# First half of batch 0's k loaded as float32 on another queue and cast by its permutes; permutes of batch 1 ordered later

**Chip, cores, metric.** One core of a Trainium2 chip. Times are device microseconds (us) of one execution.

## The reference

```python
kv  = k^T @ v                          # per batch and head: 8 batches, 8 heads, 576 rows, 64 columns
out = q @ kv                           # per batch and head
x   = out / sqrt(mean(out**2, -1) + 1e-6) * g_norm      # laid out as [8, 576, 512]
xn  = (x - mu) / sqrt(var + 1e-6) * g_ln                    # over the 512 columns
y   = x + relu(xn @ w_ch1) @ w_ch2                          # 512 -> 2048 -> 512
```

(Shortened to formulas. All inputs and the output are float32; the kernel multiplies in bfloat16.)

## The kernel before

It is written as a list of steps. Each has an engine, an estimated duration, a key and dependencies; a small scheduler in Python simulates the engines and fixes the order in which each engine's instructions are issued. So an edit of a duration or a `lag` changes the order of instructions, not their waits. The parts that matter (cuts marked):

```python
PARTS = ((0, 4), (4, 8))           # halves of the 8 heads
SPLIT_STORE = (23, 25)
...
def ready(s): ...                  # d.done + (s.lag if d is a DMA): when the plan thinks s may run
...
# SyncE queue: two small rows of scales first
row = [add("SP", 0.4, 1.4, -99, [], lambda x=x, f=f: nc.sync.dma_start(scales[:, f], ...)) ...]
# PE spreads them over 128 partitions: the two "scale matmuls"
def spread(f): nc.tensor.matmul(ps, lhsT=ones, rhs=scales[:, f], ...)
...
# GpSimd (POOL) queue: loads that cast float32 to bfloat16, one behind the other
pool_load(("k", 0, 0), load_kv(kb, k, 0, 0, 4), rate6)        # k, heads 0 to 3
pool_load(("v", 0, 0), load_kv(vb, v, 0, 0, 4), rate6)        # v, heads 0 to 3
pool_load(("k", 0, 4), load_kv(kb, k, 0, 4, 8), rate6)
pool_load(("q", 0, 0, 0), load_slot(qp[0], q, 0, 0, 0, 4), rate1)
pool_load(("v", 0, 4), ...); pool_load(("v", 0, 6), ...)      # v, the last four heads
...
pool_load(("q", 0, 1), ...); load_w(0, 1)                     # first weight of w_ch1
pool_load(("q", 0, 2), ...); load_w(1, 1)                     # q slot 2, second weight
...
# permutes: [row, head, t, d] -> [row, t, head, d], bf16 to bf16
for i, (h0, h1) in enumerate(PARTS):
    k0p.append(add("DVE", ..., load["k", 0, h0], lambda ...: k_permute(nc.vector, 0, h0, h1)))
...
# PE fills its waiting time ahead of the first feed-forward matmul with dummy matmuls (idle_ps)
```

The order on PE is: dummy matmuls, scale matmuls, the kv groups of batch 0 (three, as v arrives), q transposes, out, transposes of x, then the feed-forward matmuls.

## Time and profile before

| kernel before | value |
|---|---|
| time, median of 3 | 293.01 us (292.86 to 293.27) |
| span of the profile | 291.03 us |
| first kv group starts | 7.57 us |
| first feed-forward matmul starts | 17.24 us |
| last matmul ends | 287.57 us |

The text below shows the lines that carry this. Two lines that it does not show turn out to matter. They are from the timeline of PE in the kernel before (start, duration, engine, line, operation, count), just behind the first feed-forward group:

```profile
18.30 0.68 PE L579 MATMUL xT_ps<-identity,xc 128*128 128x128 bf16 x4
18.82 3.74 PE L629 MATMUL mm_ps<-xT,w 128*128 128x128 bf16 x64
```

and from the view of one tile, the second weight (the one `w` load issued in that stretch; the last line is issue to landing):

```profile
L354 POOL DMA_DIRECT2D w<-in_moe_w_ch_dram x1: 782/782/782, 9.6 to 9.6; - x1
...
DMA to landing us min/median/max: 9.1/9.1/9.1
```

The weight was issued at 9.63 and landed at 18.73; the second feed-forward group starts at 18.82. No wait is listed there, and yet that group could start at most 0.09 us earlier.

### The profile page before, as it was taken

The page shows a single profiled execution, that of the slowest core. Times are in us where ns is not written, and L with a number is a line of the kernel's source. Part 1 is how long each engine was busy: PE and PEld are TensorE (multiplying, and loading weights), DVE is VectorE, ACT ScalarE, POOL GpSimd, SP SyncE. Part 2 cuts the span into 40 slices and gives each one's busy share as a digit, 9 for nine tenths or more (in the row PEclk, how much of TensorE's full clock was granted, in tenths as well). Part 3 has the DMA queues.
Part 4 walks back from the last instruction along what each step waited for, and adds up shares of the span by engine and source line. Part 5 has one row for each costly group of instructions (what it writes and reads, how often), then busy time and mean ns, then how long its engine had stood idle before and what let it go on. Part 6 is the DMA issues. An engine that isn't in the chain of part 4 may idle for free.

```text
span 291.0 us, 5193 instructions
## 1 busy us (share of the span) xinstructions
PE 283.3 (97%) x2046; PEld 162.0 (56%) x2074; DVE 165.0 (57%) x362; ACT 142.5 (49%) x288; POOL 66.3 (23%) x93
## 2 busy tenths in 40 slices
PE   8899999999999999999999999999999999999995
PEld 6779845977645445444544445444544444444444
DVE  2596139487973997556755775477557755320022
ACT  2379954788756512761276126612761177016400
POOL 8974221008209005404060405000000000000000
PEclk9999999999999999999999999999999999999999
DMA  6999999959999989996999299912101310120012
GB/s 95 186 199 205 204 199 181 240 94 96 183 220 92 171 117 186 142 190 127 169 93 199 62 202 108 182 55 93 54 18 56 90 54 18 58 91 15 2 72 73
DMA packets 108716, 35.60 MB, mean 122 GB/s; under 512 B 87187, under 2 KB 104467, under 8 KB 108692
## 3 DMA queue, kind: packets, MB, share of 16 engines
q0 software_dynamic: 72624, 18.35, 65.9%
q1 hardware_dynamic: 35828, 16.79, 25.7%
q8 instruction: 16, 0.26, 0.4%
q10 hardware_dynamic: 240, 0.13, 0.2%
q14 instruction: 8, 0.07, 0.1%
HBM read 36.70 MB, written 9.44 MB: 159 GB/s over the span
## 4 chain that ended last, share of the span: by engine, by line
PE 85%; DMA 7%; POOL 6%; issue 1%; ACT 0%; DVE 0%; POOLq 0%
PE mm_ps L663 41%; PE mm_ps L644 33%; DMA qb<-in_q_dram 7%; PE mm_ps L629 5%; PE out_ps L484 3%; PE kv_ps L461 2%; POOL qp L270 1%; POOL w L354 1%; POOL vb L249 1%; POOL kb L249 1%; PE xT_ps L579 1%; POOL w L356 1%; PE qT_ps L420 0%; ACT qp L400 0%; POOL identity masks.py:197 0%
## 5 line engine op out<-in xcount | busy, mean ns | idle before, releaser
L663 PE MATMUL mm_ps<-w,m 128*128 128x512 bf16 (+2 forms) x592 | 128.1, 367 | 0.7
L644 PE MATMUL mm_ps<-xT,w 128*128 128x512 bf16 x436 | 100.0, 379 | 0.6
L651 ACT ACTIVATE m<-mm_ps 128x512 bf16<-128x512 f32 x112 | 66.8, 598 | 50.7 <-PE mm_ps L644 48.4
L663 PEld LDWEIGHTS <-m 128*128 128x128 bf16 x608 | 57.2, 98 | 60.6
L644 PEld LDWEIGHTS <-w 128*128 128x128 bf16 x448 | 43.1, 98 | 48.8
L519 DVE TENSOR_REDUCE ss<-sq 128x8 f32<-128x512 f32 (+1 forms) x37 | 24.8, 669 | 48.1 <-ACT sq L510 48.0
L670 DVE SCALAR_TENSOR_TENSOR x<-mm_ps,rstd,x 128x512 f32<-128x512 f32 (+2 forms) x38 | 27.3, 720 | 40.5 <-PE mm_ps L663 40.5
L510 ACT ACTIVATE sq<-out_ps 128x512 f32<-128x512 f32 (+1 forms) x37 | 21.6, 585 | 45.5 <-PE out_ps L484 45.5
L629 PE MATMUL mm_ps<-xT,w 128*128 128x128 bf16 x512 | 30.5, 219 | 0.0
L629 PEld LDWEIGHTS <-w 128*128 128x128 bf16 x512 | 29.2, 98 | 0.7
L572 DVE SCALAR_TENSOR_TENSOR xc<-x,mv,gl 128x512 bf16<-128x512 f32 (+1 forms) x38 | 27.3, 723 | 1.2
L514 DVE TENSOR_TENSOR xg<-out_ps,gn 128x512 f32<-128x512 f32 x34 | 23.2, 683 | 0.2
L636 ACT ACTIVATE m<-mm_ps 128x512 bf16<-128x512 f32 x32 | 18.5, 600 | 3.1 <-PE mm_ps L629 2.9
L751 POOL COPY mark<-xT 128x1 bf16<-128x1 bf16 x15 | 6.4, 425 | 56.8 <-DMA xT<-xc 51.2
L523 ACT ACTIVATE rms<-ss,eps_attn 128x8 f32<-128x8 f32 (+1 forms) x37 | 11.1, 301 | 14.5 <-DVE ss L519 14.4
L550 DVE TENSOR_TENSOR x<-xg,inv 128x512 f32<-128x512 f32 x24 | 16.6, 692 | 0.8
L566 DVE BATCH_NORM_STATS2 stats<-x 128x6 f32<-128x512 f32 x24 | 16.6, 690 | 0.5
L484 PEld LDWEIGHTS <-qT 128*128 128x128 bf16 x160 | 11.4, 98 | 6.5 <-ACT qT L400 0.2
L484 PE MATMUL out_ps<-kv_pack,qT 128*128 128x128 bf16 x160 | 14.5, 219 | 0.3
L472 DVE CAST kv_pack<-kv_ps 64x256 bf16<-64x256 f32 x14 | 5.9, 422 | 11.9 <-PE kv_ps L461 11.8
L461 PEld LDWEIGHTS <-kp 128*128 128x128 bf16 (+1 forms) x168 | 10.4, 100 | 2.4 <-DMA vb<-in_v_dram 0.4
L277 POOL DMA_DIRECT2D qp<-in_q_dram x5 | 11.2, 2235 | 0.8 <-issue 0.8
(69 smaller groups left out, 182.9 us busy)
## 6 DMA issues: line engine op xcount, KB each, us to landing
out_dram<-x SPq DMA_DIRECT2D x30, 256.0 KB, 2.9
w<-in_moe_w_ch_dram POOLq DMA_DIRECT2D x8, 512.0 KB, 12.0
vb<-in_v_dram POOLq DMA_DIRECT2D x6, 512.0 KB, 10.9
kp<-in_k_dram POOLq DMA_DIRECT2D x5, 512.0 KB, 8.5
qp<-in_q_dram POOLq DMA_DIRECT2D x5, 512.0 KB, 10.1
out_dram<-x SPq DMA_DIRECT2D x10, 128.0 KB, 2.3
qb<-in_q_dram POOLq DMA_DIRECT2D x2, 512.0 KB, 18.4
qp<-in_q_dram POOLq DMA_DIRECT2D x10, 64.0 KB, 9.1
```

The lines of the kernel that those rows point to most:

```text
L484: nc.tensor.matmul(o3[:, hp, :], lhsT=att[b]["qT"][:, 4 * t + hp, :], rhs=kv_pack[b % 3][:, hp, :], start=(i == 0), stop=(i == len(bs) - 1))
L510: nc.scalar.activation(sq[:, h0:h1, :], st[n]["ps", h0][:, h0:h1, :], func=AF.Square)
L514: nc.vector.tensor_mul(xg[:, h0:h1, :], st[n]["ps", h0][:, h0:h1, :], gn.to_broadcast([128, h1 - h0, D]))
L519: nc.vector.tensor_reduce(ss[:, h0:h1, :], st[n]["sq"][:, h0:h1, :], axis=AX.X, op=ALU.add)
L550: nc.vector.tensor_mul(x, xg, inv)
L572: nc.vector.scalar_tensor_tensor(xc[:, f0:f1], in0=st[n]["x"][:, f0:f1], scalar=blk[m]["mv"][:, i, 0:1], in1=gl[:, f0:f1], op0=ALU.subtrac ...
L629: nc.tensor.matmul(ps[:, d, :], lhsT=w1[c][:, kk, d * 128:(d + 1) * 128], rhs=blk[m]["xT"][:, kk, i * 128:(i + 1) * 128], start=(kk == 0), ...
L636: nc.scalar.activation(st[n]["m1"][:, c, :, :], st[n]["m1ps", c], func=AF.Relu)
L644: nc.tensor.matmul(ps, lhsT=w1[c][:, kk, d * 128:(d + 1) * 128], rhs=blk[m]["xT"][:, kk, :], start=(kk == 0), stop=(kk == nKm - 1))
L651: nc.scalar.activation(blk[m]["m1", c][:, d, :], blk[m]["m1ps", g], func=AF.Relu)
L663: nc.tensor.matmul(st[n]["m2ps", f0], lhsT=m1_piece(n, c, d), rhs=w2[c][:, d, f0:f1], start=(c == 0 and d == 0), stop=(c == 3 and d == 3))
L670: nc.vector.scalar_tensor_tensor(x[:, f0:f1], in0=st[n]["m2ps", f0], scalar=blk[m]["rstd"][:, i, :], in1=x[:, f0:f1], op0=ALU.mult, op1=AL ...
```

## The change

The intent: POOL's queue is the stream that every early step waits for, and the DMA engines are nearly empty in the first 3 us. So k's first half goes on the SyncE queue, which starts sooner. The new loads do not cast (the prediction says why), so the data arrive as float32 (in a buffer that batch 1 needs later), and the permute, which runs anyway, does the cast. The scales stand behind it in the SyncE queue. A `lag` of 0.7 us makes the plan expect batch 1's k and q later, so that other work is placed ahead of their transposes.

```diff
-    SPLIT_STORE = (23, 25)
+    SPLIT_STORE = ()
-        server = 3.7
+        server = 4.0
+    k_first = kb[1][:, :].bitcast(f32).rearrange("p (h t d) -> p h t d", h=4, t=6)
+    for h0 in (0, 2):
+        load["k", 0, h0] = [add("SP", 0.5, 3.3, -102, [], lambda h0=h0: nc.sync.dma_start(
+            k_first[0:96, h0:h0 + 2, :, :].rearrange("p h t d -> p h (t d)"),
+            k[0, h0:h0 + 2, 0:576, :].rearrange("h (p t) d -> p h (t d)", t=6)))]
     row = [...]                                  # the scales, unchanged, now behind the two loads
-    pool_load(("k", 0, 0), load_kv(kb, k, 0, 0, 4), rate6)
-        src = kv_view(kb, b)
+        src = k_first[0:96] if b == 0 and h1 <= 4 else kv_view(kb, b)
-    for i, (h0, h1) in enumerate(PARTS):
-        k0p.append(add("DVE", ..., load["k", 0, h0], ... k_permute(nc.vector, 0, h0, h1)))
+    k0p.append([add("DVE", ..., load["k", 0, 0], lambda: k_permute(nc.vector, 0, 0, 2)),
+                add("ACT", ..., load["k", 0, 2], lambda: k_permute(nc.scalar, 0, 2, 4))])
+    k0p.append([add("DVE", ..., load["k", 0, 4], lambda: k_permute(nc.vector, 0, 4, 8))])
-    (batch 1) ... k_permute(nc.scalar, 1, h0, h1)))
+    (batch 1) ... k_permute(nc.scalar, 1, h0, h1), lag=0.7))
-    (batch 1) ... q_permute(nc.scalar, 1, t, t + 1))
+    (batch 1) ... q_permute(nc.scalar, 1, t, t + 1), lag=0.7)
```

The `lag` moves more than batch 1: on PE the kv group of batch 2 now comes a whole feed-forward tile earlier.

More of the change, by code (lines that the diff above doesn't have):

```diff
@@ L680 @@
     k0p = []
-    for i, (h0, h1) in enumerate(PARTS):
-        k0p.append(add("DVE", 0.13 * (h1 - h0) + 0.07, 0.13 * (h1 - h0) + 0.15, -80 + i, load["k", 0, h0],
-                       lambda h0=h0, h1=h1: k_permute(nc.vector, 0, h0, h1)))
+    k0p.append([add("DVE", *dve_cost(768), -80, load["k", 0, 0], lambda: k_permute(nc.vector, 0, 0, 2)),
+                add("ACT", *act_cost(768), -80, load["k", 0, 2], lambda: k_permute(nc.scalar, 0, 2, 4))])
+    k0p.append([add("DVE", 0.59, 0.67, -79, load["k", 0, 4], lambda: k_permute(nc.vector, 0, 4, 8))])
     for h0, h1 in PARTS:
@@ L696 @@
         w = (h1 - h0) / 8
-        s = add("PE", 1.36 * w, 1.36 * w + 0.25, -60 + i, load["v", 0, h0] + [k0p[h0 // 4]],
+        s = add("PE", 1.36 * w, 1.36 * w + 0.25, -60 + i, load["v", 0, h0] + k0p[h0 // 4],
                 lambda hps=hps, i=i: kv_mm(0, hps), alloc="kvt")
@@ L727, in plan_batch @@
                 kperm.append(add("ACT", 1.2, 1.35, p - 18, load["k", 1],
-                                 lambda h0=h0, h1=h1: k_permute(nc.scalar, 1, h0, h1)))
+                                 lambda h0=h0, h1=h1: k_permute(nc.scalar, 1, h0, h1), lag=0.7))
             for t in range(5):
@@ L732, in plan_batch @@
                     qperm = add("ACT", *act_cost(512), key, load["q", 1],
-                                lambda t=t: q_permute(nc.scalar, 1, t, t + 1))
+                                lambda t=t: q_permute(nc.scalar, 1, t, t + 1), lag=0.7)
                     qread = qperm
```

## The prediction

> **What bounds the kernel now.** I read the page first, then PE's waits, the timeline of the first 20 us, the landing time of each early load (a tile asked for in a window that holds one issue of it), and PE's timeline from 32 to 72 us.
>
> The page and PE's waits:
>
> ```profile
> PE 283.3 (97%) x2046; PEld 162.0 (56%) x2074; DVE 165.0 (57%) x362; ACT 142.5 (49%) x288; POOL 66.3 (23%) x93
> PEclk9999999999999999999999999999999999999999
> DMA  6999999959999989996999299912101310120012
> ...
> PE idle_ps L1007 <- DVE eps_ln L208: 1.0, 1, 1.0
> PE qT_ps L420 <- DMA qp<-in_q_dram: 0.5, 1, 0.5
> PE xT_ps L579 <- DVE xc L572: 0.4, 2, 0.2
> PE kv_ps L461 <- DMA vb<-in_v_dram: 0.2, 1, 0.2
> PE kv_ps L461 <- DVE qT L402: 0.2, 1, 0.2
> PE out_ps L499 <- DVE sums L546: 0.2, 1, 0.2
> ```
>
> TensorE is busy 97% of the span at full clock, and all its listed waits lie in the first 19 us; later there are only stops of some 0.05 to 0.2 us. The first useful matmul of the feed-forward part (w times xT, L629) starts at 17.24 us and the last matmul ends at 287.58. In between lie 270.3 us of matmuls that no arrival interrupts. So the time is: start of the first L629 matmul (17.24) + 270.3 + last eviction and store (3.45) + what the measured time has over the span (293.01 - 291.0 = 2.0). The change keeps the work in the second term. It can win only by moving 17.24, and lose only by opening a wait in the second term.
>
> What sets 17.24 is the prologue, in the timeline:
>
> ```profile
> 1.31 0.82 POOL L249 DMA_DIRECT2D kb<-in_k_dram  x1 [0.86 <-POOLq L1039]
> 2.39 2.39 PE L325 MATMUL scale_ps<-scales,ones 1*128 1x512 f32 x4
> 6.05 0.60 DVE L402 COPY kp<-kb 96x1536 bf16<-96x1536 bf16 x1 [0.68 <-DMA kb<-in_k_dram]
> 7.57 1.09 PE L461 MATMUL kv_ps<-vb,kp 96*128 96x128 bf16 x12
> 9.35 0.69 DVE L402 COPY kp<-kb 96x1536 bf16<-96x1536 bf16 x1 [0.23 <-DMA kb<-in_k_dram]
> 11.38 0.51 PE L461 MATMUL kv_ps<-vb,kp 96*128 96x128 bf16 x6 [0.22 <-DMA vb<-in_v_dram]
> 15.93 0.40 PE L420 MATMUL qT_ps<-identity,qp 128*128 128x128 bf16 x4
> 17.24 1.06 PE L629 MATMUL mm_ps<-xT,w 128*128 128x128 bf16 x16
> ```
>
> (Start, duration, engine, line, operation; the bracket is idle time and what ended it.) Each step starts where a load lands: k's first half 6.03, v's first half 7.45, k's second half 9.32, q slot 0 9.79, v's last two heads 11.34. From the last one it is a chain of DVE, ACT and PE steps of 5.9 us to 17.24. The loads stand in one POOL queue and land one behind the other: 7.45 - 6.03 = 1.42 us for half of v, 96 x 4 x 384 x 4 bytes = 590 KB read, and 2.53 us (18.73 to 21.26) for a 1 MiB weight, both 415 GB/s. The queue is thus limited by transfer, and the two windows
>
> ```profile
> 2.00:3.00 1.00, 1.00 (x6) 0.69 (x4) 0.00 (x0) 0.23 (x2) 1.00 (x3) 1.00 0.18 12
> 3.00:4.00 1.00, 1.00 (x2) 0.33 (x1) 0.00 (x0) 0.00 (x0) 1.00 (x2) 1.00 0.74 82
> ```
>
> (last two columns: DMA share and GB/s) show that it hardly moves anything before about 3.3 us. The DMA engines are empty for the first 3 us, then full till past 60.
>
> **What the Trainium skill says.** "DMA: Bandwidth & Descriptors", section "SWDGE vs HWDGE vs iDMA": a load that casts must go through GpSimd[...]. That is why k must come as float32 and be cast by its permute. The same page, "Issuing engines are not separate DMA queues": all queues share the same 16 DMA engines, so a second queue brings no bandwidth. The trace agrees that the engines are the limit (share 0.9 and up from 4 us). What the new queue can bring is an earlier start: "Anatomy of one DMA" gives a SWDGE transfer about 2 us fixed. Here POOL's first load is issued at 1.31, and its bytes (6.03 less 1.42 less about 1 us of completion) start near 3.6; the SyncE loads of the scales, issued at 0.75, have been used by 2.39. "VectorE: DVE Perf Modes", tier table: a float32 copy in SBUF runs at 2x where bf16 runs at 4x (1227 against 693 ns for 2048 elements). The bf16 permute of 1536 elements took 0.60 us here; the float32 speed no run has shown yet.
>
> **The change part by part.**
> 1. k's first half leaves the POOL queue: 1.42 us of transfer less ahead of every other POOL load, and one issue (0.8 us) less. v's first half becomes POOL's first load.
> 2. The same 590 KB go on SyncE from 0.75 us, in two loads. With the scales' delay (about 1.2 us to bytes) they move from about 2.0 to 3.4 at full rate, perhaps 3.9. POOL's bytes start between 3.3 and 3.6, so 0 to 0.5 us of the 1.42 collide. Net: every POOL load lands 0.9 to 1.4 us earlier, middle 1.15. v first half 6.3, k second half 8.2, last v 10.2, q slot 2 14.7.
> 3. The permute becomes two, 768 float32 elements each: DVE about 0.5 us by the skill's table, ACT about 0.7 (estimate: half of the 1.26 us median of its 1536-element k permutes), from about 4 to 5 us, when both engines idle. Beside other work: no cost.
> 4. The scales now stand behind k in the SyncE queue. Estimate: they land near 4.3 instead of before 2.4. PE is in order: 21 filler matmuls, the two scale matmuls (2.39 to 4.71, 2.3 us), 6 fillers (0.65), then kv. So 4.3 + 2.3 + 0.65 = 7.3 for the first kv group, against 7.57, though v is there at 6.3. The first kv group gains only 0.3, and with it the DVE steps behind it (mask, second k permute, qT copy: some 0.3 to 0.45).
> 5. The last kv group waits for v at 10.2, for the second permute (about 9.6) and for the first out group ahead of it (about 10.5): about 10.6 against 11.38. Its mask, the reduction behind it, and the second half's out follow 0.7 to 0.8 us earlier than the 11.93, 12.14 and 12.47 of now. The rest to the first L629 keeps its order. First L629 near 16.4: minus 0.85.
> 6. Order later. The two q transposes of batch 1 are moved one m2 group (4 x 216 ns = 0.86 us) later, since q of batch 1 lands at 38.39 and the transposes now start at 39.09 practically on its heels. With PE 0.85 early and the group inserted, they come at 39.1 - 0.85 + 0.86, less the 0.15 to 0.3 waited now: 38.9; q lands at 37.2, permutes of 0.6 us each end at 38.5. No wait. But kv of batch 2 moves ahead of a whole feed-forward tile: it comes at 49.93 - 0.85 + 4 x 0.89 + 0.22 = 52.9, and its last v piece lands now at 53.41, then at about 52.3. And the out groups of tiles 9 and 10 move 1.1 us ahead as well, from 68.56 to 66.6, with q of batch 2 turned by about 66.5 now. Both have little slack: I allow 0.1 us for them.
> 7. Unsplit stores of two tiles: four stores become two, near 180 us, nobody waits for them. Zero.
>
> Sum: -0.85 + 0.1 = -0.75; 293.01 - 0.75 = 292.26, rounded to 292.2.
>
> **The rivals.**
> (a) The scales become the bound: if they land at 5.5 rather than 4.3, the first kv group starts at 8.5, the gain of the prologue is eaten, and the time stays at 293.0 or goes slightly above. For it: they are queued behind 590 KB, PE in order waits for them. Against it: they are 2 KB, and later steps have about 0.8 us slack.
> (b) Everything moves with the DMA stream: the early kv group is not on the path (its PE fillers hide it) and 17.24 moves by the full 1.15 or even 1.4: 291.6 to 291.9.
> (c) The gain is given back at 53 or 66.6 us, as DMA transposes and stores of the same stretch (share 0.9 and up) do not move with the loads: q of batch 2 is issued only after ACT's last permute, which the changed order does not make earlier. Then PE waits up to 0.5 us there: 292.7.
> (d) k collides with v so fully that the POOL stream gains only 0.5 us: 292.5.
>
> **Range and chances.** The mechanisms span -1.4 to about +0.1, the repeats 0.4 us. Range 291.6 to 292.9. 2% is 5.9 us; nothing here reaches that: faster 0.01, same 0.98, slower 0.01.
>
> **What would show it.** Right: the first L629 matmul at 16.2 to 16.6, v's last heads landing near 10.2, scale matmuls starting at 4 to 4.6, no PE wait above 0.2 us after 20 us, and 270.3 us from there to the last matmul. Wrong: scale matmuls after 5 us, or a first L629 outside 15.8 to 17.0; or a PE wait on v or qT at 53 or 66 us; or a PE total that changes.

## The result, and the profile after

Ratios here are the mean time of one kernel's fast runs over that of the other's of the same rounds, so not quite the ratio of the medians.

| | before | after |
|---|---|---|
| median of 4 runs each, us | 292.94 (292.79 to 293.27) | 293.87 (293.69 to 294.51) |
| ratio, 95% interval | | 1.0034 [1.0017, 1.0052] |
| span of the profile | 291.03 | 292.08 |
| scale matmuls start | 2.39 | 5.38 |
| first kv group starts | 7.57 | 8.36 |
| v's last heads land | 11.34 | 11.60 |
| first feed-forward matmul | 17.24 | 17.70 |
| second weight lands | 18.73 | 19.15 |
| second feed-forward group | 18.82 | 19.29 |
| from there to the end of the last matmul | 268.75 | 269.33 |

Some 0.9 us slower where 0.75 faster was predicted. Two of PE's waits in the changed kernel are new (total, times, longest):

```profile
PE scale_ps L332 <- DMA scales<-in_moe_g_ln_dram: 2.0, 1, 2.0
PE kv_ps L467 <- DMA v<-in_v_dram: 0.6, 1, 0.6
```

They are for the scales in the prologue, and for v of batch 2 much later. The span's +1.05 us adds up from two places: the second feed-forward group starts 0.47 later, and the stretch behind it is 0.58 longer. That the listed wait for v is 0.58 too is chance. Counted from start to start (between 53.88 and 54.84 below stand four matmuls of 56 ns), PE lost 0.74 us there, and another 0.20 among the out matmuls at 60.87. The kernel before lost neither, but 0.31 us at 39.09, ahead of q's transposes of batch 1: the stop that the later order was to avoid, and did. What follows the last matmul is 3.46 us in both. The timeline of the changed kernel:

```profile
0.75 0.90 SPq L321 DMA_DIRECT2D kb<-in_k_dram  x2
4.14 0.56 DVE L408 CAST kp<-kb 96x768 bf16<-96x768 f32 x1 [2.46 <-DMA kb<-in_k_dram]
5.32 0.83 ACT L406 CAST kp<-kb 96x768 bf16<-96x768 f32 x1 [3.08 <-DMA kb<-in_k_dram]
5.38 2.36 PE L332 MATMUL scale_ps<-scales,ones 1*128 1x512 f32 x4 [1.96 <-DMA scales<-in_moe_g_ln_dram]
8.36 1.44 PE L467 MATMUL kv_ps<-vb,kp 96*128 96x128 bf16 x12
9.59 1.59 PE L1013 MATMUL idle_ps<-blank 128*128 128x128 bf16 x13
11.86 0.50 PE L467 MATMUL kv_ps<-vb,kp 96*128 96x128 bf16 x6
17.70 1.06 PE L635 MATMUL mm_ps<-xT,w 128*128 128x128 bf16 x16
...
53.88 0.39 PE L467 MATMUL kv_ps<-vb,kp 128*128 128x128 bf16 x4
54.84 0.22 PE L467 MATMUL kv_ps<-v,kp 128*128 128x128 bf16 x1 [0.58 <-DMA v<-in_v_dram]
```

The casts are cheap (0.56 and 0.83 us, at times when both engines are free). The two k loads land at 4.12 and 5.30, the scales only behind them. The last kv group, at 11.86, is later than before (11.38), and from it the chain to the feed-forward part is the old one: 11.86 + 5.84 = 17.70. It was not waiting for v, whose last heads had landed at 11.60: from the scale matmuls at 5.38 on, PE runs up to it without a listed wait, at half speed until 11.1 (the 13 dummy matmuls at 9.59 took 1.59 us; 0.89 before). The same windows that are shown of the kernel before (the last two columns are DMA share and GB/s) say what became of the empty time:

```profile
2.00:3.00 1.00, 1.00 (x12) 1.00 (x10) 0.00 (x0) 0.23 (x2) 1.00 (x3) 1.00 0.93 263
3.00:4.00 1.00, 0.42 (x4) 0.15 (x2) 0.00 (x0) 0.00 (x0) 1.00 (x2) 1.00 1.09 269
```

It is filled, as intended, with 263 and 269 GB/s. Then why do POOL's loads not land earlier? And the last entries: where before's PE did its kv group of batch 2 at 58.61 us, the new order has it at 53.88, ahead of its data.

### The profile page after: what moved, and what is told of

Read it like the earlier page. It is cut to its first block, busy times and chain, and to the rows that moved or that the text cites. A ratio compares the mean times of both kernels' runs of the same rounds, so it can differ in the third digit from the quotient of the medians.

```text
span 292.1 us, 5201 instructions
## 1 busy us (share of the span) xinstructions
PE 284.2 (97%) x2062; PEld 161.9 (55%) x2062; DVE 164.6 (56%) x362; ACT 143.1 (49%) x289; POOL 64.9 (22%) x92
## 4 chain that ended last, share of the span: by engine, by line
PE 82%; DMA 13%; POOL 1%; DVE 1%; issue 1%; ACT 0%; SPq 0%; DVEq 0%
PE mm_ps L669 38%; PE mm_ps L650 33%; DMA qb<-in_q_dram 7%; DMA v<-in_v_dram 5%; PE mm_ps L635 4%; PE kv_ps L467 3%; PE out_ps L490 3%; DMA scales<-in_moe_g_ln_dram 1%; PE idle_ps L1013 1%; PE scale_ps L332 1%; POOL w L363 0%; PE xT_ps L585 0%; SPq L321 0%; POOL kb L251 0%; POOL vb L251 0%
## 5 line engine op out<-in xcount | busy, mean ns | idle before, releaser
L669 PE MATMUL mm_ps<-w,m 128*128 128x512 bf16 (+2 forms) x608 | 129.8, 368 | 0.0
L529 ACT ACTIVATE rms<-ss,eps_attn 128x8 f32<-128x8 f32 (+1 forms) x37 | 11.1, 300 | 11.0 <-DVE ss L525 10.9
L467 PE MATMUL kv_ps<-vb,kp 128*128 128x128 bf16 (+1 forms) x144 | 11.3, 227 | 0.0
## 6 DMA issues: line engine op xcount, KB each, us to landing
w<-in_moe_w_ch_dram POOLq DMA_DIRECT2D x8, 512.0 KB, 11.9
vb<-in_v_dram POOLq DMA_DIRECT2D x6, 512.0 KB, 10.9
```

Of the source, the lines that this page charges most:

```text
L467: nc.tensor.matmul(ps[:, hp, :], lhsT=kp[b % 2][p, t, 2 * hp:2 * hp + 2, :].rearrange("p h d -> p (h d)"), rhs=(v5[b % 2][:, 2 * hp:2 * hp ...
L669: nc.tensor.matmul(st[n]["m2ps", f0], lhsT=m1_piece(n, c, d), rhs=w2[c][:, d, f0:f1], start=(c == 0 and d == 0), stop=(c == 3 and d == 3))
```

## The experiments

Fifteen runs. Three causes stood against each other: the scales stand behind k; the new order brings batch 2's kv ahead of its v; or the load itself costs the POOL stream what it saves. Unless said, an edit is to the changed kernel and its result is correct. Executions of the kernel before on the same chips ranged over 292.6 to 294.8 us, so a single ratio resolves some 0.3%, about 0.8 us; the profiles, with their waits, resolve more. But one profile is one execution, and the landings of the same code differ by over a microsecond from one to another, as the repeats show.

**Scales on ACT's queue.**

```diff
-    row = [add("SP", ...: nc.sync.dma_start(scales[:, f], ...)) ...]
+    nc.scalar.dma_start(scales[:, f], ...)     # both, as ACT's first instructions
```

> The changed kernel, but the two scale loads leave the SyncE queue (where they stood behind k) and are issued by ScalarE first of all; nothing else moves. Theory A (the late scales cost the prologue: PE stands still 2.0 us, and then runs 12 kv and 13 filler matmuls at about 0.105 us each instead of 0.06 to 0.08): scale matmuls start near 3.3 instead of 5.38, the filler matmuls behind the first kv group run at 0.056 us again, first feed-forward matmul 0.2 to 0.5 us earlier than 17.70. Theory B (the GpSimd loads themselves land later because k now uses the DMA engines before and beside them): v's first half still lands at 8.3 and its last heads at 11.6, the first kv group still starts at 8.3, and the first feed-forward matmul gains at most 0.25 us, so that it does not get back to the 17.24 of the kernel before.

Scale matmuls at 3.35, first kv group 6.86, v's last heads 10.93; but the first feed-forward matmul only at 17.30 and the second weight at 18.68. 293.62 against 293.5 us, ratio 1.0003 [0.9985, 1.0020]. The wait for the scales is gone (a real loss of the change), and the gain that should then show does not. One reason stands in the profile: PE was at half speed until 11.8 (the 13 dummy matmuls took 1.59 us again, not the expected 0.056 each), so the last kv group started 0.33 us earlier than before but took 0.84 us for 0.51.

**kv of batch 2 placed later again.**

```diff
+    moved = [adone[2]["kvmm"], adone[2]["kv"][0].deps[0], adone[2]["kv"][0]]
+    # taken out of the order, put in behind the second feed-forward group of tile 5
```

> The changed kernel, but the kv group of batch 2 stands after two feed-forward groups of tile 5 (2.2 us of PE work) instead of before them. Theory C (0.6 to 0.75 us of the loss is that kv group's wait for v's last rows): no PE wait on v at 54 us, span 291.4 (0.6 to 0.75 less than 292.1), first feed-forward matmul unchanged at 17.7. Rival: the DMA stream is behind as a whole, and the wait turns up at a later load, out groups of tiles 9 and 10 near 66 us above all: span unchanged, 292.1.

The wait for v went, but PE then stopped at about 61 us twice, some 0.3 us each from start to start, ahead of out matmuls; the first feed-forward matmul, expected unchanged, came at 18.17. 293.97 us, ratio 1.0013 [0.9993, 1.0032]. What this one move gives back is not resolved.

**Both.**

> Both edits. If the two losses are separate and add, the span is 291.4 less what the first edit alone gains (0.0 to 0.5): 290.9 to 291.4, that is the kernel before (291.0) or slightly better or worse. If the first wins more than 0.5 us, it is a kernel better than both.

294.36 us, ratio 1.0023 [1.0003, 1.0043]: the repair of both listed waits did not help. In this profile v's first half landed at 8.72, over a microsecond later than the 7.45 of the kernel before, and PE waited 2.3 us for it. That was the first hint that the load itself is the matter.

**The new order alone** (on the kernel before: `lag=0.7` and unsplit stores), run twice.

> The kernel before (k by GpSimd with cast, scales alone on SyncE) with only the later order of batch 1's permutes and the unsplit stores, which gives the changed kernel's order on every engine from 32 us on. Theory C: prologue unchanged at 17.24, and a PE wait of v's last rows at the kv group of batch 2, of 0.2 to 0.7 us (PE gets there 0.46 us earlier than in the changed kernel, the loads maybe too): time 0.2 to 0.7 us above before. Rival (the order does no harm by itself; v's last rows were late only through the new k load): no wait, time equal to before within 0.1 us.

> The old k load with the new order, a second time: prologue as before (17.2 to 17.5), kv group of batch 2 waits for v's last rows by 0.5 to 1.8 us whenever these land after 53.7, so 270.7 to 271.4 us to the last matmul: time 0.3 to 1.0 us above before. Were the wait seen in the first profile of it a chance, 270.4 and a time equal to before.

294.01, ratio 1.0005 [0.9986, 1.0025]; again 293.93, 1.0005 [0.9977, 1.0032]. The first profile has the wait, alone, in a kernel without the new load:

```profile
53.68 0.39 PE L461 MATMUL kv_ps<-vb,kp 128*128 128x128 bf16 x4
55.26 0.22 PE L461 MATMUL kv_ps<-v,kp 128*128 128x128 bf16 x1 [1.19 <-DMA v<-in_v_dram]
```

The second has not: there v's last rows landed at 52.76 instead of 55.22, and two small waits of 0.3 and 0.2 us stand instead. So the wait for v comes and goes (0 to 1.2 us) with the landing of those rows, but the stretch from the second feed-forward group to the last matmul's end is longer in both: 269.83 and 269.44, against 268.75 before.

**The load alone**: the changed kernel with the lag taken back, which gives the order of before on every engine (only the two stores stay unsplit).

```diff
-  ... k_permute(nc.scalar, 1, h0, h1), lag=0.7))   ... q_permute(nc.scalar, 1, t, t + 1), lag=0.7)
+  ... k_permute(nc.scalar, 1, h0, h1), lag=0.0))   ... q_permute(nc.scalar, 1, t, t + 1), lag=0.0)
```

> The new k load with the kernel before's order of everything from 32 us on (the 0.7 us lag set to 0). Theory: the prologue loses 0.2 to 0.9 us as in the changed kernel (first feed-forward matmul 17.3 to 18.2), the rest loses nothing (270.2 to 270.5 us to the last matmul): time 0.2 to 0.9 us above before, and under the changed kernel's. Rival (the order is not to blame; any order waits for the late loads): 270.7 or more.

294.03, ratio 1.0007 [0.998, 1.0034]. Scales at 5.17, first feed-forward matmul 18.65, second group 20.25: with the load alone the prologue is later. How much of that is the load this one profile does not say: PE was at half speed until 13.7, and came to the last kv group 0.70 us after v's last heads had landed (11.65).

**The float32 load added, nothing removed** (the kernel before, scales on ACT, plus both SyncE loads into a buffer that nobody reads).

```diff
+    for h0 in (0, 2):
+        (add("SP", ...: nc.sync.dma_start(k_first[0:96, h0:h0 + 2, ...], k[0, h0:h0 + 2, ...])))
```

> The kernel before (all of k by GpSimd) with the two float32 loads of the changed kernel added on SyncE into a buffer that is not read then, and the scales issued by ScalarE so that they do not queue behind them. It measures the collision alone. In the kernel before, k's first half landed at 6.03 and v's last heads at 11.34. Theory B (the load costs the GpSimd stream about its whole transfer time or more, so that the earlier start brings nothing): k's first half lands 1.0 to 2.0 us later (7.0 to 8.0), v's last heads at 12.4 to 13.5, time 1 to 2 us above before. Rival, as my prediction had it (the load moves mostly in the empty time before 3.6 us): k's first half at most 0.5 us later (6.5), v's last heads at 11.8, time at most 0.5 above before.

296.12, ratio 1.0083 [1.0052, 1.0114]. k's first half, by POOL, lands at 8.52 instead of 6.03, v's last heads at 13.53 instead of 11.34, the second weight at 20.59 instead of 18.73. PE's timeline:

```profile
10.20 1.44 PE L467 MATMUL kv_ps<-vb,kp 96*128 96x128 bf16 x12 [2.53 <-DMA vb<-in_v_dram]
20.81 1.06 PE L635 MATMUL mm_ps<-xT,w 128*128 128x128 bf16 x16
```

So the load is not hidden in the empty time at all. Summed over the packets of the trace, POOL's queue reached the bytes of v's last heads at 11.9 us here against 10.2 to 10.6 in four profiles with k in that queue and no SyncE load: a delay of 1.3 to 1.7 us, about the 1.42 that the same bytes took in POOL's own queue.

**The load taken away** (scales on ACT; a memset in place of k's first half, so the result is wrong, relative error 0.25).

```diff
-        load["k", 0, h0] = [add("SP", ...: nc.sync.dma_start(k_first[...], k[0, ...]))]
+    nc.vector.memset(kb[1][0:96, :], 0.0)
```

> The changed kernel with the scales on ScalarE and without k's SyncE loads: a memset of the buffer stands in for them, so the result is wrong on purpose. The GpSimd stream meets nothing. If the schedule could use it: v's first half lands at 6.0, its last heads at 9.9, the first feed-forward matmul starts at 16.0 to 16.5, time 0.8 to 1.2 us under before. If the prologue is held by something else (PE's fillers, the slow clock of PE, DVE): loads as said, first feed-forward matmul at 17.0 or later.

292.91, ratio 0.9983 [0.9946, 1.0019]. v's first half lands at 5.62 and its last heads at 9.01, 2.3 us earlier than before the change. And still the first feed-forward matmul gains only 0.4 us, and the span is longer (292.55). (The profiled execution was the slowest of the four, 294.33; two others, 292.05 and 292.47, are below every run of the kernel before on this chip.) The reasons, from PE's timeline of this run:

```profile
15.04 0.29 PE L584 MATMUL xT_ps<-identity,xc 128*128 128x128 bf16 x2 [0.17 <-DVE xc L577]
15.53 0.40 PE L425 MATMUL qT_ps<-identity,qp 128*128 128x128 bf16 x4
16.83 1.06 PE L634 MATMUL mm_ps<-xT,w 128*128 128x128 bf16 x16
18.30 0.89 PE L634 MATMUL mm_ps<-xT,w 128*128 128x128 bf16 x13
55.41 0.22 PE L466 MATMUL kv_ps<-v,kp 128*128 128x128 bf16 x1 [1.82 <-DMA v<-in_v_dram]
```

The four q transposes wait for q slot 2, which landed at 15.48, and PE, in order, comes to the first feed-forward matmul 1.35 us after that landing. In the kernel before it is 15.89 + 1.35 = 17.24, in the order-alone run 16.11 + 1.35 = 17.46. This second bound, in the kernel before level with the kv chain (11.38 + 5.84 = 17.22), the prediction had missed. And what was won at the front was lost at 55 us, waiting 1.8 us for v.

**Half of the load** (heads 0 and 1 by SyncE, 2 and 3 by POOL's queue; scales on ACT).

```diff
-    for h0 in (0, 2):
+    for h0 in (0,):
+    pool_load(("k", 0, 2), load_kv(kb, k, 0, 2, 4), rate6)     # first in POOL's queue
```

> Half the dose, scales on ScalarE: heads 0 and 1 of k by SyncE as float32, heads 2 and 3 by GpSimd with the cast, first in its queue. Theory B: 295 KB less collide, their transfer ends near 3.3 before GpSimd's stream is at full rate (4.0 to 4.5), so that most of the 0.7 us is won: v's first half lands near 6.8 to 7.2, first feed-forward matmul 0.2 to 0.6 us before 17.24, time 0.2 to 0.6 under before. If what counts is that two queues run at all (first GpSimd packet later by 0.7 us, unequal progress of the 16 engines), v's first half lands at 7.4 or later, as before, and nothing is won.

293.89, ratio 1.0022 [0.9993, 1.0051]. POOL's packets start at 2.9 us, nearly as without the load (2.8), and v's first half lands at 6.88 instead of 7.45; v's last heads, at 11.48, gain nothing. First feed-forward matmul 17.47, second group 19.00, 0.8 us of wait for v of batch 2.

**Repeats**: the changed kernel twice, the kernel before once.

> The changed kernel unchanged, to see what of its profile repeats. If the loads of the prologue scatter from run to run, v's first half lands anywhere from 6.8 to 8.7 as in the four profiles so far; the scales' wait on PE (1.4 and 2.0 us in two profiles) and the collision of the first GpSimd packet (3.5 to 3.6 us) repeat; the wait of the batch 2 kv group varies between 0 and 0.75. Time 0.5 to 1.0 us above before.

> The changed kernel once more, on the same chip as its two halves: time 0.5 to 1.1 us above before; scales' wait of PE 1.4 to 2.0 us; first feed-forward matmul 17.4 to 17.8; 270.6 to 271.1 us to the last matmul.

> The kernel before, unchanged, as a kernel of its own: how far two sets of runs of one program differ, and a second profile of it. Ratio 1.000 within 0.0025. First feed-forward matmul at 17.2 to 17.5, 270.3 to 270.6 us from it to the last matmul, no wait of PE at the kv group of batch 2.

Changed: 294.3, ratio 1.0018 [0.9991, 1.0045], and 293.93, 1.0017 [0.9992, 1.0043]. Before against itself: 0.9993 [0.9965, 1.0021]. Scale matmuls 4.92 and 4.77; first feed-forward matmul 17.41 and 18.69. The 0.6 us wait for v came in neither (v's last rows landed at 52.2 and 53.2); one of them had 0.5 us at 60 us, for q's transposes, instead.

The second profile of the kernel before has its first feed-forward matmul at 18.13 (17.2 to 17.5 was expected) and its second group at 19.25, though v's last heads landed early, at 10.90. q slot 2 landed at 16.77, 0.9 us later than in the first profile, and PE waited for it:

```profile
16.82 0.40 PE L420 MATMUL qT_ps<-identity,qp 128*128 128x128 bf16 x4 [1.14 <-DMA qp<-in_q_dram]
18.13 1.06 PE L629 MATMUL mm_ps<-xT,w 128*128 128x128 bf16 x16
```

So this second bound is real in the kernel before itself (16.77 + 1.36 = 18.13), and one profile of a front that scatters by 0.9 us settles little. All profiles of the four variants, by the start of the second feed-forward group and the stretch from there to the last matmul's end:

| | second group starts | stretch behind it |
|---|---|---|
| k by POOL, order before | 18.82, 19.25 | 268.75, 268.52 |
| k by POOL, order later | 19.00, 18.89 | 269.83, 269.44 |
| k by SyncE, order before | 20.25 | 268.78 |
| k by SyncE, order later | 19.29, 19.00, 20.28 | 269.33, 269.03, 268.38 |

The load shows in the first column (with much scatter) and the order in the second; where the front is very late (20.28), the later order has no stop left to show.

On the one chip that ran all four variants, the mean times are:

| | order before | order later |
|---|---|---|
| k by POOL | 293.40 (18 runs, with the repeat) | 293.73 (6) |
| k by SyncE | 293.77 (6) | 294.08 (12) |

Load +0.37, order +0.33, both +0.68 us. Each single step is within the noise (standard errors of these means: 0.14 to 0.25 us); that they add up to the whole is suggestive, and the direction agrees with the profiles.

**q slot 2 moved ahead of the first weight** (the kernel without the load).

```diff
+    pool_load(("q", 0, 2), load_slot(qp[0], q, 0, 2), rate1)
     load_w(0, 1)
-    pool_load(("q", 0, 2), load_slot(qp[0], q, 0, 2), rate1)
```

> As e6_no_load (no SyncE load of k, memset in its place, wrong on purpose), with q slot 2's load issued ahead of the first weight's. Theory (q slot 2 is the second bound of the prologue: in e6 its landing at 15.48 plus 1.35 is the first feed-forward matmul at 16.83): q slot 2 lands near 11.3, the first weight near 15.6, and the first feed-forward matmul starts at 15.9 to 16.4. Rival (the chain of DVE, ACT and PE steps sets it, slowed by the cold PE clock): 16.8 again. In both the wait for v of batch 2 at 55 us stays, so I expect little or no gain of the time: ratio to before 0.996 to 1.002.

293.08, ratio 0.9985 [0.9958, 1.0012]. The first feed-forward matmul came at 15.57, 1.26 us earlier than with q slot 2 behind. Most of that is not q slot 2's: the first x transpose, which does not wait for it, came at 13.91 instead of 15.04, with PE at full speed from 8.9 us in this profile and only from 11.4 in the other. From that transpose to the first feed-forward matmul it is 1.66 us here, 1.79 in the other, and 2.90 in the second profile of the kernel before; so q slot 2 had cost 0.13 us in the run without the load and 1.24 in that repeat. PE's timeline goes on:

```profile
13.91 0.29 PE L584 MATMUL xT_ps<-identity,xc 128*128 128x128 bf16 x2 [0.17 <-DVE xc L577]
15.57 1.06 PE L634 MATMUL mm_ps<-xT,w 128*128 128x128 bf16 x16
16.64 0.68 PE L584 MATMUL xT_ps<-identity,xc 128*128 128x128 bf16 x4
19.16 5.04 PE L634 MATMUL mm_ps<-xT,w 128*128 128x128 bf16 x59 [1.84 <-DMA w<-in_moe_w_ch_dram]
```

Now it waits 1.84 us for the second weight, landed at 19.12, and after that stop the matmuls start 107 ns apart instead of 56 until 22.5: PE had fallen back to half speed. There is a third bound behind the second, and this explains the lines of the kernel before: its second group starts 0.09 us after its second weight.

**Scales on ACT and the order of before, new load kept**; and the same with q slot 2 ahead of the first weight.

> The changed kernel with the scales issued on ACT (as e1) and with the order later as before the change (as x1). If the losses are the late scales and the later order, and nothing else, this is level with the kernel before or 0.2 us better: scale matmuls at 3.4, first feed-forward matmul 17.0 to 17.4, 270.3 us from there, no wait on v near 54 us, ratio 0.998 to 1.001. Rival (the SyncE load itself costs, by taking transfer time from the POOL queue and by raggedness of the landings): last v heads land at 11.3 or later, first feed-forward matmul 17.4 or later, ratio 1.001 to 1.003.

> x3 with q slot 2 ahead of the first weight: both bounds of the prologue relaxed. If q slot 2 was the only thing that kept x3 from gaining: first feed-forward matmul 0.3 us earlier than in x3 (16.7 to 17.1), ratio to before 0.998. If the kv chain is the bound or the first weight becomes it (landing near 16.2 to 16.8): 17.2 to 17.8, level with x3.

293.69, ratio 1.0011 [0.9991, 1.0031], and 293.32, ratio 1.0007 [0.9985, 1.0030]; both level with before. In the first, PE's timeline and one of its waits:

```profile
17.27 1.06 PE L635 MATMUL mm_ps<-xT,w 128*128 128x128 bf16 x16
18.30 0.68 PE L585 MATMUL xT_ps<-identity,xc 128*128 128x128 bf16 x4
19.12 1.07 PE L635 MATMUL mm_ps<-xT,w 128*128 128x128 bf16 x16
...
39.77 0.40 PE L426 MATMUL qT_ps<-identity,qp 128*128 128x128 bf16 x4 [0.52 <-ACT qp L406]
```

First matmul 17.27, as before; the second group held by its weight (19.07); and 0.52 us for q of batch 1, which landed at 39.07. This is the wait that the later order is meant to avoid: it saves up to half a microsecond at 39 us and risks up to 1.2 at 54 (1.8 in the run without the load). In the second run v's first half happened to land at 8.59 and everything followed, with PE at half speed until 14.7 (first matmul 19.24), so its profile says nothing about q slot 2. No variant beat the kernel before.

## Why the prediction was wrong, step by step

The frame held: span = start of the feed-forward part + its matmuls + 3.46 us, and its warning signs (scale matmuls after 5 us, a first matmul above 17.0, a wait on v at 53 us) are what the profile shows. Looking at the second group is better still. From its start to the last matmul's end, three profiles (the repeat with first matmul at 18.69, the added load, the last variant) give exactly 268.38 us. What the others have over that are later waits and stops: 0.37 before, 0.95 in the changed kernel, 1.45 with the order alone, 2.30 without the load.

1. *k leaves the queue* (−1.42 us): true as far as it goes. Without a SyncE load, v's last heads landed 2.3 and 2.0 us earlier in the two profiles of it.
2. *The bytes move in empty time, net gain 0.9 to 1.4*: **this step failed, and it is the first cause of the missing gain.** I took the 415 GB/s of POOL's stream for the new load. That rate counts float32 bytes read by loads that write half as many; a plain copy writes all 590 KB. In the windows from 2 to 4 us the DMA engines moved 263 and 269 GB/s (counted as written), so 590 KB take about 2.2 us (an estimate from these), not 1.42; in the packet records k runs from 1.8 to between 4.3 and 4.8 us. Whether the doubled bytes or a slow start set that rate, no run tells apart. Nor was the time empty for as long as I read: POOL's first packet goes at 2.8 us in the kernel before, not at the 3.3 to 3.6 of my estimate, while more than half of k still has to move. With the new load that packet comes at 3.5 or later, and the added load delayed the queue by all of its old transfer time. What is left of the gain is a queue that is on average 0.4 us ahead (v's last heads' bytes reached at 10.0 in the mean of nine profiles, at 10.4 in that of four). Even that did not reach PE: with the SyncE load the landings of v's first half to its last heads come 0.8 to 2.5 us behind the moment when the queue as a whole had moved enough, without it 0.6 to 1.0. The last heads landed at 10.88 to 12.10 in nine profiles with the load (mean 11.5), 10.90 to 11.41 in four without (mean 11.2); predicted was 10.2.
3. *The permutes are free*: right, 0.56 and 0.83 us for 0.5 and 0.7.
4. *Scales at 4.3*: mis-sized, 4.8 to 5.4 in the five profiles with this queue order, behind a k that took longer than I had allowed (step 2). PE stands still for 1.3 to 2.0 us. Half speed makes that dearer, and "full clock" in my first paragraph overlooked it: the 13 dummy matmuls behind the first kv group took 0.89 us before and 1.59 in the changed kernel. But they took 1.59 in the first order-alone profile too, where nothing waits for the scales, so half speed is not shown to come from the change.
5. *The last kv group at 10.6, first matmul at 16.4*: measured 11.86 and 17.70. (The 0.78 us that this step finds for the last kv group became 0.85 for the first matmul without a reason given; and the sum, 292.26, rounds to 292.3.) I had v as what this group waits for. In the four profiles with k in POOL's queue it is, and the group starts 0.04 to 0.05 us after v's last heads land; in the five with the scales behind k it starts 0.26 to 0.75 us after, because PE, held up by the scales and at half speed until 10.9 us or later, is not there yet. But had v come at 10.2 and PE been ready, 16.4 could still not have been reached: q slot 2 (15.5 to 16.8 us where it stands behind the first weight, without the added load; predicted 14.7) and the second weight (18.73 to 19.05 in the four profiles with k in POOL's queue, 18.35 to 19.60 in eight with the load) are two more bounds at nearly the same place. In its first profile the tuned kernel had its three early bounds within 0.1 us of one another. Total bytes read up to the second weight are the same in either version, so that bound moves only by what the stream as a whole gains.
6. *The later order, 0.1 us*: mis-sized, the second cause. I put v's last rows at 52.3; they land between 52.2 and 55.4, on no schedule that I can read from the front of the kernel. The group now asks for them at 53.2 to 54.9; before it did at 58.6, with some 5 us to spare. When the group was moved back, other small stops came at 61 us. That the DMA stream paces the kernel up to about there, so that whatever comes earlier waits, fits this but was not tested.
7. *Stores*: nothing seen, right.

Of the rivals, (a) is nearly what the changed kernel's first profile shows (scales at 5.4, first kv group at 8.4, the gain of the prologue gone), and (c) came true beside it; (b), the full gain, nowhere. (d) gave 0.5 us for the POOL stream, near the 0.4 that the queue as a whole gained, but wrongly assumed that the landings follow.

**What stays open**: why the landings scatter and lag more with the second queue active (no run shows which of the 16 DMA engines lag); why PE leaves half speed anywhere from 8.1 to 16.4 us, while the chain from the last kv group to the first feed-forward matmul takes 5.84 us where PE is at full speed by then and 6.25 to 6.5 in five profiles where it is not; and the exact share of load, late scales and order in the loss (ratios 1.0034, 1.0018 and 1.0017 in three comparisons, 0.5 to 1.0 us), since each alone is below what the timed rounds resolve. That the load is not hidden and that the change is slower are shown; the split of the loss is only supported.

## What to carry to other kernels

In a tuned pipeline, look for the next bound behind the one you relax: ask of every step near the path how long before its use its data landed, also where no wait is listed (here 0.09 us). When a load moves to another queue of the same DMA engines, do not take its rate from the old queue: add it alone once to see what it costs the others, and see what stands behind it in its new queue. An order that avoids one wait spends the slack of something else; find out whose. And profile the old kernel twice before reading a few tenths out of its front: here the second profile differed by 0.9 us.

## What the Trainium skill lacked or had wrong

- "DMA: Bandwidth & Descriptors" was right that another queue brings no bandwidth ("Issuing engines are not separate DMA queues"): adding the float32 load moved POOL's second weight from 18.73 to 20.59 us. Its bandwidth table is for one stream and has no rate for a float32 copy beside casting loads; here some 265 GB/s moved between 2 and 4 us with the float32 load, and 186 GB/s (as written, half of what is read) in the casting stream of the kernel before from 5 to 16 us.
- The same page gives no figure for how far a load's landing falls behind its queue's bytes while a second queue starts: here 0.8 to 2.5 us, against 0.6 to 1.0 without.
- "TensorE: Matmul & The Clock Gate", section "What's actually happening", gives a free-running idle window of about 3.4 us before the clock halves. Here a stop of 1.84 us at 17.3 us was followed by 3.4 us at half speed, and one of 1.82 us at 53.6 us by none. That the start varies from run to run agrees, but full speed came between 8.1 and 16.4 us in these profiles, and at 8.1 and 9.7 in two of the same kernel. From the first matmul at 1.0 us that is over 7 us, where the page's warm-up is some 3.4 us of sustained work; whether the one-row scale matmuls in between count as work, no run here tells.
